# Attention and Sinkhorn-routed experts on one core: x kept by rows in DRAM and turned by DMA, weights in small loads

## The chip, the cores and the metric

The kernel runs on one core of one Trainium2 chip. The metric is the device time of one execution in microseconds (us). Three executions of the kernel before took 1023.87 us in the median (1021.98 to 1028.93). A further one was profiled, and every row below is from it.

## The reference

Attention over 8 batches with 8 heads of size 64: 512 local and 32 global tokens each. A local query sees the local keys within 32 positions and all global keys; a global query sees all keys. The result is x with N = 8*544 = 4352 rows and D = 512 columns. Then eight experts with weights from a Sinkhorn iteration:

```python
x = attn_out.transpose(0, 2, 1, 3).reshape(B * S, H * D)
P = np.exp(x @ w_gate - (x @ w_gate).max())
for _ in range(8):
    P /= P.sum(1, keepdims=True) + 1e-09
    P /= P.sum(0, keepdims=True) + 1e-09
    P *= N / E
for e in range(E):                      # E = 8, F = 1024
    h = np.maximum(x @ w1[e], 0.0)
    out += P[:, e:e + 1] * (h @ w2[e])
```

P depends on all rows of x, so no expert's share can be weighted before the attention of the last batch is done. Since P is positive, P * relu(x w1) w2 = relu((P x) w1) w2.

## The kernel before, in words

**Order of the work.** Every piece of work is an `op` with an engine, a cost in us, a key and dependencies (L123). `run_schedule` (L153) takes again and again the op that can start first by these costs, the smallest key first among equals, and issues it. So the order of instructions on each engine is fixed when the program is built, and each engine works through its own list in order: an instruction that waits holds all behind it on that engine. Loads and stores issued from SyncE stand in the queue SP, those from GpSimd in POOL.

**Attention** (L213 to L331). Work goes by 32 pairs of heads, four to a batch. Inputs of a batch are loaded on SP into single buffers (`load`, L202), cast by DVE, turned by PE (`transposes`, L222), and evicted; then scores, exponentials on ACT, masks on DVE, and `attend` (L268). `normalise` (L297) divides on DVE and writes x by rows, tokens on partitions. `back` (L329) turns the four 128x128 blocks of a pair with PE into the bank `xo`, and a copy (EB, L520) writes them into `xT`, a tile that holds all of x by columns in SBUF. The global rows go the same way by `flip` (L335, L526) and ACT (L527). `gate` (L339) makes the logits of all complete 128-row tiles after each batch, `exp_gate` their exponentials.

**Expert 0** (L388 to L422) runs unweighted and dense on groups of 512 tokens: `h_unit` makes the hidden layer, `y_unit` the second layer, `evac_y` copies it out, `store_y` (L422) stores it on POOL to `y0d` in DRAM. Its ops have keys from 1000 on, so PE takes them where attention leaves it free. Its weights are loaded by `load_w0` (L540).

**Sinkhorn** (L645 to L661) is a chain on DVE with a column sum on PE (L656) in each round. The result `P_nat` is turned by PE in three parts (`turn`, L667) and stored to `ptd`, so that it can be loaded back with the 256 tokens of a group along the free axis and spread over all partitions (`pb`, L696). x by columns is also stored, in 17 groups of 256 tokens (`xTd`, L610).

**Expert stage** (L818 on). Experts 1 to 7 run in two passes, (1, 2, 3) and (4, 5, 6, 7); a unit is one group of 256 tokens with one expert, 51 + 68 = 119 units. Both layers are done with seven products instead of eight (a Strassen-like scheme): the weights are combined by DVE (`combine_w1`, `combine_w2`, four operations of 128x1024 each), so is x (`prep`, L698). For each unit `prep` multiplies the group's x by `pb` (two DVE operations, L708) and makes three sums. Layer 1 of unit u (`add_layer1`, L847) is planned from TU*u on, TU = 6.2 us, and layer 2 (`add_layer2`, L880) two units later. Weighted x has three buffers (`xp`); unit k's buffer is that of unit k-3, whose last reader is product P3. Layer 2 accumulates over the experts of a pass in four PSUM banks; they start from the sum of the pass before (`load_o` L767, `seed` L773), which is stored by `store_o` (L935), both on SP.

The PSUM banks of the products of layer 1 come free with the attention pools (`open_late`, L614); those of layer 2 only when expert 0 is done (L808 to L815). All of the expert stage is planned after a first `run_schedule()` (L807) has issued attention, expert 0 and Sinkhorn.

**Weights** of experts 1 to 7 are loaded on POOL as four transfers each (`load_w1` L81, `load_w2` L89), fp32 in DRAM and fp16 in SBUF. Experts 1 and 2 are loaded near the end of attention, 3 when its pools are freed, 4 and 5 at unit 8 and 20 of the plan, 6 and 7 at the end of the first pass into the buffers of 1 and 2 (L956 to L961).

Of the kernel before, what the change touches and what calls it, by code (L numbers as in the profile page):

```python
# [9 lines left out]
FP16 = mybir.dt.float16  # L10
# [7 lines left out]
def kernel(  # L18
# [51 lines left out]
    identity32 = persist.tile([P, P], FP32)  # L70
    xT = fill.tile([P, DP, NTOK], FP16, bufs=1)
# [6 lines left out]
    xTd = dram.tile([GN, P, DP, 256], FP16)  # L78
    ws = {}

    def load_w1(e, pool, tag=""):  # L81
        w1r = pool.tile([P, 4, DK, F // 2], FP16, tag="w1r" + tag, bufs=1, name="w1r")
        src = moe_w1[e].rearrange("(dko dki) f -> dki dko f", dki=P)
        for f in (0, 1):
            nc.gpsimd.dma_start(out=w1r[:, 2 * f : 2 * f + 2].rearrange("p a k x -> p (a k) x"),
                                in_=src[:, :, F // 2 * f : F // 2 * (f + 1)])
        ws[e] = [w1r, None, None]

    def load_w2(e, pool, tag=""):  # L89
        wb = ws[e][1] = pool.tile([P, 7, FK, Dhalf], FP16, tag="wb" + tag, bufs=1, name="wb")  # L90
        src = moe_w2[e].rearrange("(fko fki) d -> fki fko d", fki=P)
        for c in (0, 1):
            nc.gpsimd.dma_start(out=wb[:, 2 * c : 2 * c + 2].rearrange("p a k x -> p (a k) x"),
                                in_=src[:, :, Dhalf * c : Dhalf * (c + 1)])
# [101 lines left out]
    qkT, ugk, u_, xns, ogs, pts, pss, pgs, pos_, pqs, hTs, phs, pys = ({} for _ in range(13))  # L196
# [100 lines left out]
    def normalise(p):  # L297
        pv = pos_[p][:, :, 0 : NM * VC].rearrange("p i (t c) -> p i t c", c=VC)
        rz = wk.tile([P, 2, NM], FP32, tag="rz", name="rz")
        nc.vector.reciprocal(out=rz, in_=pv[:, :, :, Dh])  # L300
        t = xns[p] = wk.tile([P, NM, 2, Dh], FP16, tag="xn", bufs=3, name="xn")
        nc.vector.tensor_tensor(out=t.rearrange("p t i d -> p i t d"), in0=pv[:, :, :, 0:Dh],
                                in1=rz.unsqueeze(3).broadcast_to([P, 2, NM, Dh]), op=ALU.mult)

    pog = gbank[:, 256 : 256 + VC]
    xo = gbank[:, 0:256].bitcast(FP16)
    ptg = gbank[:, 384 : 384 + 2 * Sg].rearrange("p (a s) -> p a s", s=Sg)
# [15 lines left out]
    def normalise_g(b, hh):  # L323
        rg = wk.tile([P, 1], FP32, tag="rg", name="rg")
        nc.vector.reciprocal(out=rg, in_=pog[:, Dh:VC])
        t = ogs[b, hh] = wk.tile([P, Dh], FP16, tag="og", name="og")
        nc.vector.tensor_scalar(out=t, in0=pog[:, 0:Dh], scalar1=rg[:, 0:1], scalar2=None, op0=ALU.mult)

    def back(p):  # L329
        for m in range(NM):  # L330
            nc.tensor.transpose(xo[:, P * m : P * (m + 1)], xns[p][:, m, :, :], identity)  # L331
# [7 lines left out]
    def gate(t0, t1):  # L339
        for to in range(t0, t1):  # L340
            for dk in range(DP):
                nc.tensor.matmul(pl[:, (to - t0) * E : (to - t0 + 1) * E], xT[:, dk, P * to : P * (to + 1)],
                                 w_gate_sb[:, dk, :], start=(dk == 0), stop=(dk == DP - 1))

    def exp_gate(t0, t1):
        nc.scalar.activation(out=K_nat[:, t0:t1, :].rearrange("p t e -> p (t e)"),
                             in_=pl[:, 0 : (t1 - t0) * E], func=AF.Exp)
# [37 lines left out]
    GT = 4  # L385
    groups = [(t, min(GT, TO - t)) for t in range(0, TO, GT)]

    def h_unit(g, fm, half):  # L388
# [6 lines left out]
        for dk in range(2 * half, 2 * half + 2):  # L395
            nc.tensor.matmul(phs[g, fm][:, 0:TG], w1_0[:, dk, P * fm : P * (fm + 1)], xT[:, dk, P * g0 : P * g0 + TG],  # L396
# [19 lines left out]
    def evac_y(eng, g, c):  # L416
        t = yss[g, c] = (late["ys"] if "ys" in late else fill).tile([P, D], FP32, tag="ys", bufs=5 if "ys" in late else 2,
# [8 lines left out]
    make_identity(nc, identity32)  # L426
# [22 lines left out]
    T, EQ, EK, SC, X, M, GK, XG, A, N, AG, NG, BK, EB, FL, EF, GA, GE, GO, XS = ({} for _ in range(20))  # L449
# [62 lines left out]
    def add_attend(p):  # L512
# [5 lines left out]
        N[p] = op("DVE", 0.85, lambda: normalise(p), k + 0.2, uses=[A[p]], alloc=("xn", 3))  # L518
        BK[p] = op("PE", 0.24, lambda: back(p), k + 0.3, uses=[N[p]], alloc=("xo", 1), lat=PEL)
        EB[p] = op(either(0.49, 0.61), 0, lambda eng: copy_on(eng, xT[:, hp, S_tok * b + Sg : S_tok * (b + 1)], xo), k + 0.3,  # L520
                   uses=[BK[p]])
        if hp % 2 == 1:
            AG[b, hh] = op("PE", 0.36, lambda: attend_g(b, hh), k + 0.25, [A[p], XS[b // 2]],
                           uses=[X[p, 0, 0], X[p - 1, 0, 0]], alloc=("pog", 1), lat=PEL)
            NG[b, hh] = op("DVE", 0.4, lambda: normalise_g(b, hh), k + 0.25, uses=[AG[b, hh]], alloc=("og", 2))
            FL[b, hh] = op("PE", 0.15, lambda: flip(ptg, ogs[b, hh]), k + 0.35, uses=[NG[b, hh]], alloc=("ptg", 1), lat=PEL)  # L526
            EF[b, hh] = op("ACT", 0.15, lambda: nc.scalar.copy(  # L527
                out=xT[:, 2 * hh : 2 * hh + 2, S_tok * b : S_tok * b + Sg], in_=ptg), k + 0.35, uses=[FL[b, hh]])

    S_tok = Sg + Sl  # L530
# [7 lines left out]
    tick = const.tile([P, 1], FP32)  # L538

    def load_w0():  # L540
        nc.gpsimd.tensor_copy(out=tick, in_=stage[1, "q"][:, 0, 0:1])
# [6 lines left out]
    ready_b, sched_gate = {}, 0  # L548
    for b in range(B):
# [17 lines left out]
        t0, t1 = sched_gate, (S_tok * (b + 1)) // P  # L567
        sched_gate = t1
        ready_b[b] = [EB[p] for p in range(HP * b, HP * (b + 1))] + [EF[b, 0], EF[b, 1]]
        GA[b] = op("PE", 0.55, lambda t0=t0, t1=t1: gate(t0, t1), HP * (b + 1) + 0.6, ready_b[b], alloc=("pl", 1), lat=PEL)  # L570
# [424 lines left out]
```

## Time and profile before

| what | value |
|---|---|
| profiled execution | 1021.38 us |
| its span | 1019.7 us, mean granted clock 0.99 |
| last gate's exponential starts | 187.9 us |
| P_nat written | 219.6 us |
| first product of the expert stage | 260.6 us |
| last matmul starts | 1013.6 us |
| DMA packets | 127530, 119.18 MB |
| SP's queue (hardware) | 91.13 MB, 29.3% of the 16 engines' span |
| POOL's queue (software) | 25.70 MB, 13.4% |

In the 40 slices of the profile each slice is 25.5 us and each digit a tenth of busy time. PE's busy time counts matmuls with modelled, overlapping ends; the weight loads (PEld) take about 0.1 us each and tell better how dense PE's work is. Attention fills slices 0 to 7, the rest of expert 0 with Sinkhorn beside it 7 to 10, the expert stage the remainder.

### The profile page before, as it was taken

How to read it: one execution, taken by the hardware profiler on the slowest of the kernel's cores; microseconds unless marked ns; L12 is line 12 of the kernel's file. 1: busy time of each engine (PE TensorE's matmuls, PEld its weight loads, DVE VectorE, ACT ScalarE, POOL GpSimd, SP SyncE). 2: the span in 40 equal slices, each digit the busy share in tenths (PEclk: the TensorE clock that was granted, in tenths of full speed). 3: DMA queues.
4: the chain of work that ended last, by engine and by line, in shares of the span. 5: the costliest groups of instructions: out<-in, count | busy, mean ns of one | idle time of the engine just before them, and what ended most of it. 6: DMA issues, size and time to landing. Idle time of an engine off the chain costs nothing. (4 is left out here: it accounts for less than half of the span.)

```text
span 1019.7 us, 30644 instructions
## 1 busy us (share of the span) xinstructions
PE 980.2 (96%) x12921; PEld 829.9 (81%) x12921; DVE 884.6 (87%) x2058; ACT 671.7 (66%) x1306; POOL 51.8 (5%) x89
## 2 busy tenths in 40 slices
PE   5999999889999999999999889999999999999997
PEld 3556555434799999999999878999999999999997
DVE  5577776581599999999999899999999999999996
ACT  4678877434677766676776656666666666666664
POOL 2000130211300000000000100000000000000000
PEclk9799999989999999999999999999999999999999
DMA  9979696732962232232322891222222222222211
GB/s 272 256 219 307 193 215 126 144 103 100 229 140 85 94 94 89 90 94 93 108 73 79 153 195 60 88 73 74 74 74 73 75 74 74 74 75 73 75 43 43
DMA packets 127530, 119.18 MB, mean 117 GB/s; under 512 B 17424, under 2 KB 102944, under 8 KB 127392
## 3 DMA queue, kind: packets, MB, share of 16 engines
q1 hardware_dynamic: 99040, 91.13, 29.3%
q0 software_dynamic: 26768, 25.70, 13.4%
q8 instruction: 101, 1.65, 0.7%
q10 hardware_dynamic: 1584, 0.39, 0.2%
q14 instruction: 37, 0.30, 0.1%
HBM read 102.65 MB, written 31.33 MB: 131 GB/s over the span
## 5 line engine op out<-in xcount | busy, mean ns | idle before, releaser
L740 ACT ACTIVATE h<-h 128x512 f16<-128x512 f16 x357 | 224.2, 630 | 72.0 <-DVE h L100 70.1
L726 PEld LDWEIGHTS <-w1r 128*128 128x128 f16 x3808 | 244.9, 98 | 22.6 <-issue 13.7
L726 PEld LDWEIGHTS <-w1x 128*128 128x128 f16 x2856 | 182.3, 98 | 5.3
L764 PEld LDWEIGHTS <-s 128*128 128x128 f16 x1904 | 172.4, 98 | 15.9 <-DVE s L100 0.6
L708 DVE TENSOR_TENSOR xp<-xg,pb 128x512 f16<-128x512 f16 x238 | 163.0, 686 | 15.2 <-PE Y L726 15.0
L726 PE MATMUL X<-tt,w1r 128*128 128x128 f16 x1904 | 145.1, 219 | 7.4 <-ACT u3s L737 5.8
L764 PE MATMUL acc_4639<-wb,s 128*128 128x256 f16 x952 | 142.5, 273 | 0.3 <-DVE s L100 0.3
L764 PEld LDWEIGHTS <-h 128*128 128x128 f16 x1428 | 130.0, 98 | 12.6 <-issue 1.0
L737 ACT COPY u3s<-X 128x512 f32<-128x512 f32 x119 | 69.4, 583 | 73.7 <-PE X L726 73.4
L100 DVE TENSOR_TENSOR h<-p1s,Z 128x512 f16<-128x512 f32 x119 | 81.0, 681 | 29.5 <-ACT p1s L737 27.9
L737 ACT COPY p1s<-X 128x512 f32<-128x512 f32 x119 | 69.1, 580 | 29.1 <-PE X L726 29.1
L100 DVE TENSOR_TENSOR h<-u3s,Y 128x512 f16<-128x512 f32 x119 | 81.1, 681 | 2.1 <-ACT u3s L737 2.1
L737 ACT COPY u2s<-X 128x512 f32<-128x512 f32 x119 | 68.5, 576 | 21.5 <-PE X L726 21.4
L100 DVE TENSOR_TENSOR h<-u2s,Y 128x512 f16<-128x512 f32 x119 | 81.0, 680 | 1.6 <-PE Y L726 1.6
L740 ACT ACTIVATE h<-X 128x512 f16<-128x512 f32 x119 | 70.1, 589 | 17.0 <-PE X L726 14.0
L396 PE MATMUL ph<-xT,w_0_77 128*128 128x512 f16 (+1 forms) x288 | 74.0, 374 | 1.8 <-ACT ys L200 1.1
L726 PE MATMUL X<-xp,w1r 128*128 128x128 f16 x952 | 72.6, 219 | 1.9 <-DVE xp L708 1.7
L726 PE MATMUL Z<-xp,w1r 128*128 128x128 f16 x952 | 72.6, 219 | 1.1 <-DVE h L100 1.0
L726 PE MATMUL X<-tt,w1x 128*128 128x128 f16 x952 | 72.6, 219 | 0.0
L726 PE MATMUL Y<-tt,w1x 128*128 128x128 f16 x952 | 72.6, 219 | 0.0
L726 PE MATMUL Y<-xp,w1x 128*128 128x128 f16 x952 | 72.6, 219 | 0.0
L764 PE MATMUL acc_4636<-wb,s 128*128 128x256 f16 x476 | 71.4, 273 | 0.1
(985 smaller groups left out, 1651.1 us busy)
## 6 DMA issues: line engine op xcount, KB each, us to landing
pb<-ptd SPq DMA_DIRECT2D x119, 128.0 KB, 4.1
y0d<-ys POOLq DMA_DIRECT2D x34, 256.0 KB, 3.5
xg<-xTd SPq DMA_DIRECT2D x34, 256.0 KB, 3.7
o<-y0d SPq DMA_DIRECT2D x34, 256.0 KB, 2.8
ya<-o SPq DMA_DIRECT2D x34, 256.0 KB, 2.1
o<-ya SPq DMA_DIRECT2D x34, 256.0 KB, 3.0
out_dram<-o SPq DMA_DIRECT2D x34, 256.0 KB, 2.0
qs<-in_q_l_dram SPq DMA_DIRECT2D x7, 1024.0 KB, 6.9
```

The source lines that it names most:

```text
L100: nc.vector.tensor_tensor(out=o, in0=a, in1=b_, op=ALU.add)
L396: nc.tensor.matmul(phs[g, fm][:, 0:TG], w1_0[:, dk, P * fm : P * (fm + 1)], xT[:, dk, P * g0 : P * g0 + TG], start=(dk == 0), stop=(dk == ...
L708: nc.vector.tensor_tensor(out=x[:, ks], in0=xgs[n, g][:, ks], in1=pb.unsqueeze(1).broadcast_to([P, DK, 256]), op=ALU.mult)
L726: nc.tensor.matmul(dst[:, j, :], l[:, d, P * j : P * (j + 1)], r[:, d, :], start=(first and j == 0 and d == 0), stop=(j == FK - 1 and d == ...
L737: nc.scalar.copy(out=d[k], in_=X[k])
L740: nc.scalar.activation(out=hq(k, f, t), in_=hq(k, f, t) if src is None else src, func=AF.Relu)
L764: nc.tensor.matmul(acc(i), l[:, j, :], wb[:, r, j, :], start=(e == es[0] and j == 0 and i in (1, 5)), stop=(e == es[-1] and j == FK - 1), ...
```

## The change

x is no longer kept by columns in SBUF. `normalise` writes two pairs into one tile, which POOL stores by rows to `xd` in DRAM (`store_x`), the global rows SP (`store_xg`). For gate and expert 0 each group of 512 tokens is read back with a DMA transpose on SP (`turn_group`), into three buffers; gate goes by these groups. In the expert stage a group is loaded by rows once per pass, scaled by rows with P as a scalar per partition on ACT or DVE (`scale_x`), stored to one of four DRAM buffers (`put_x`), and read back with a DMA transpose (`turn_x`). P is not turned any more.

Weights of experts 1 to 5 are loaded on POOL in 16 pieces each; before each piece POOL waits until the piece before the last has landed. In the expert stage each piece also waits for the x of a given unit. Experts 6 and 7 are first converted to fp16 in DRAM by 16 pieces each and then loaded by SP in four halves. `load_o` and `store_o` move from SP to POOL, the third seed of a group is placed after the second. Layer 1 of units 0 and 1 and the x of units 0 to 3 are planned in the first `run_schedule()`, together with expert 0.

```diff
+    def load_piece(e, i):
+        if len(landed) > 1:
+            wait_for(landed[-2])
+        if i < 8:
+            k, f = divmod(i, 2)
+            o = ws[e][0][:, 2 * f + k // DK, k % DK, :]
+            nc.gpsimd.dma_start(out=o, in_=moe_w1[e][P * k : P * (k + 1), F // 2 * f : F // 2 * (f + 1)])
+            landed.append(o[:, 0:1])
...
+    def cast_piece(e, i):
+        d, src, n = (wd1, moe_w1, D // 8) if i < 8 else (wd2, moe_w2, F // 8)
+        r = slice(n * (i % 8), n * (i % 8 + 1))
+        nc.gpsimd.dma_start(out=d[e][r], in_=src[e][r])
...
-    def back(p):
-        for m in range(NM):
-            nc.tensor.transpose(xo[:, P * m : P * (m + 1)], xns[p][:, m, :, :], identity)
+    def store_x(b, hh):
+        r0 = S_tok * b + Sg
+        nc.gpsimd.dma_start(out=xd[r0 : r0 + Sl, 4 * Dh * hh : 4 * Dh * (hh + 1)].rearrange("(m p) d -> p m d", p=P),
+                            in_=xns[2 * b + hh].rearrange("p m i d -> p m (i d)"))
...
+    def turn_group(g):
+        t0, n = groups[g]
+        xTs[g] = fill.tile([P, DP, n * P], FP16, tag="xT", bufs=3, name="xT")
+        nc.sync.dma_start_transpose(out=xTs[g], in_=xd[P * t0 : P * (t0 + n)])
...
-        BK[p] = op("PE", 0.24, lambda: back(p), k + 0.3, uses=[N[p]], alloc=("xo", 1), lat=PEL)
-        EB[p] = op(either(0.49, 0.61), 0, lambda eng: copy_on(eng, xT[:, hp, S_tok * b + Sg : S_tok * (b + 1)], xo), k + 0.3,
+            stored[b].append(op("DMA3", 0.7, lambda: store_x(b, hh), k + 0.5, uses=[N[p], N[p - 1]], lat=DMAL))
...
+                TG[g] = op("DMA", 2.0, lambda g=g: turn_group(g), k, [x for x in stored[b] + (stored[b - 1] if b else [])],
+                           alloc=("xT", 3), lat=5.5)
+                GA[g] = op("PE", 0.55, lambda g=g: gate(g), k + 0.1, alloc=("pl", 1), uses=[TG[g]], lat=PEL)
...
-        t = pbs[n, g] = late["cp"].tile([P, 4, 2, P], FP32, tag="pb", name="pb")
-        for i, e in enumerate(es):
-            nc.sync.dma_start(out=t[:, i], in_=ptd[2 * g : 2 * g + 2, e, :].unsqueeze(0).broadcast_to([P, 2, P]))
+    def scale_x(eng, k, a):
...
+        if eng == "ACT":
+            nc.scalar.activation(out=o, in_=i, func=AF.Copy, scale=w)
+        else:
+            nc.vector.tensor_scalar(out=o, in0=i, scalar1=w, scalar2=None, op0=ALU.mult)
+    def put_x(k):
+        nc.sync.dma_start(out=xsd[k % NX].rearrange("(a p) d -> p a d", p=P), in_=xss[k])
+    def turn_x(k):
+        xps[k] = late["cp"].tile([P, DP, 256], FP16, tag="xp", bufs=3, name="xp")
+        nc.sync.dma_start_transpose(out=xps[k], in_=xsd[k % NX])
...
-            nc.vector.tensor_tensor(out=x[:, ks], in0=xgs[n, g][:, ks], in1=pb.unsqueeze(1).broadcast_to([P, DK, 256]),
...
+        mk("PX", k, "DMA", 0.1, lambda: put_x(k), at + 1.0, [(("SC", 1), k)], [(("SC", 0), k)], ("xsd", NX), lat=2.3)
+        mk("TX", k, "DMA", 1.2, lambda: turn_x(k), at + TU, [], [("PX", k)], ("xp", 3), lat=2.3)
...
-                    mk("FC", nx, "ACT", 0.4, lambda: seed(*nx, 2), t + 9.0, [], [("LO", nx)])
+                    mk("FC", nx, "ACT", 0.4, lambda: seed(*nx, 2), t + 12.0, [("FA", nx)], [("LO", nx)])
...
-        mk("LO", c, "DMA", 0.2, lambda: load_o(*c), t, alloc=("o", 2), lat=2.5)
+        mk("LO", c, "DMA2", 1.5, lambda: load_o(*c), t, [("open", 0), ("y", 0), ("y", 1)], alloc=("o", 2), lat=6.0)
...
+    def load_w(e, deps, pool):
+        for i in range(16):
+            mk(("W", i), e, "DMA", 1.3, lambda i=i: (new_w(e, i, pool()), load_piece(e, i)), 900.0 + e + 0.01 * i,
+               deps if i == 0 else [(("W", i - 1), e)], lat=DMAL)
...
+    for k in range(4):
+        add_prep(k)
+    add_o(c0, 0.0)
+    for k in (0, 1):
+        add_layer1(k)
+    run_schedule()
...
+        if 4 <= u < NW:
+            add_prep(u)
+            while npc < 64 and 4 + npc * 0.66 <= u:
+                add_piece(npc, u)
+                npc += 1
```

## The prediction

> **What bounds the kernel now.** I read the page first (busy times, 40 slices), then busy time by stretch, the groups by shape, the timeline of 187 to 260 us, the waits of 500 to 570 us and the DMA issues.
>
> ```profile
> span 1019.7 us, 30644 instructions
> PE 980.2 (96%) x12921; PEld 829.9 (81%) x12921; DVE 884.6 (87%) x2058; ACT 671.7 (66%) x1306; POOL 51.8 (5%) x89
> PE   5999999889999999999999889999999999999997
> PEld 3556555434799999999999878999999999999997
> ```
>
> PE is the bound nearly everywhere; the weight loads (PEld) show where it is full in earnest: from slice 10 on, with a dip at slices 22 to 24 (about 560 to 640 us).
>
> ```profile
> 26.00:60.00 34.00, 30.95 (x468) 19.37 (x465) 22.50 (x55) 22.63 (x50) 0.40 (x1) 0.85 0.86 224
> 200.00:210.00 10.00, 5.30 (x17) 2.15 (x17) 7.01 (x17) 1.67 (x3) 0.54 (x1) 0.70 0.70 147
> 300.00:400.00 100.00, 99.91 (x1349) 93.55 (x1347) 100.00 (x237) 70.25 (x133) 0.00 (x0) 1.00 0.30 94
> 500.00:570.00 70.00, 65.51 (x884) 61.48 (x883) 63.02 (x151) 45.65 (x89) 1.50 (x2) 1.00 0.28 88
> 570.00:650.00 80.00, 75.47 (x996) 69.10 (x993) 79.02 (x183) 49.18 (x94) 4.99 (x6) 1.00 0.60 123
> 700.00:800.00 100.00, 100.00 (x1363) 94.89 (x1361) 95.26 (x225) 67.91 (x127) 0.00 (x0) 1.00 0.24 75
> ```
>
> Columns: stretch, length, PE, PEld, DVE, ACT, POOL busy with counts, granted clock, DMA share, GB/s. A unit of the expert stage has 7*8 + 7*4 = 84 matmuls; at 1363 per 100 us it takes 6.17 us, and 119 units 734 us. The stage runs from 260.4 to 1014.2, 754 us, so about 20 us are lost in it: against 13.63 per us, 300-500 lacks 2.8 us, 500-570 5.1, 570-650 6.9, the rest lies in the first 40 us and the drain.
>
> ```profile
> 202.26 0.44 DVE L643 TENSOR_TENSOR t_4156<-K_nat,rv 128x272 f32<-128x272 f32 x1
> 204.90 0.69 DVE L97 TENSOR_TENSOR wb<-wb 128x1024 f16<-128x1024 f16 x1 [2.19 <-DMA wb<-in_moe_w_dram]
> 205.51 0.62 DVE L651 TENSOR_REDUCE cp<-t_4156 128x8 f32<-128x272 f32 x1
> ...
> 206.19 0.59 PE L656 MATMUL pcs<-cp,ones_sc 128*128 128x8 f32 x2 [3.83 <-DVE cp L651]
> ```
>
> Here one weight combination stands in DVE's queue before its data, the Sinkhorn step behind it is late, and PE, in order, stands for 3.83 us at the column sum although expert 0 has work; the clock is then 0.50 from 205 to 210.
>
> ```profile
> L331 PE MATMUL gbank<-identity,xn 128*128 128x128 f16 x128 | 13.3, 230 | 3.6 <-DVE og L327 1.7 <-DVE xn L302 1.7
> L337 PE MATMUL gbank<-identity,og 128*64 128x64 f16 x32 | 3.6, 218 | 0.5 <-ACT xT L200 0.2
> L200 ACT COPY xT<-gbank 128x512 f16<-128x512 f16 x30 | 17.7, 590 | 10.0 <-PE gbank L337 6.0 <-PE gbank L331 3.8
> ...
> ACT o L781 <- DMA o<-y0d: 9.3, 4, 4.0
> ...
> PE X L726 <- ACT u3s L737: 4.5, 4, 3.0
> ...
> y0d<-ys POOLq DMA_DIRECT2D x34, 256.0 KB, 3.5
> xg<-xTd SPq DMA_DIRECT2D x34, 256.0 KB, 3.7
> xTd<-xT SPq DMA_DIRECT2D x17, 256.0 KB, 5.4
> ...
> w1r<-in_moe_w_dram POOLq DMA_DIRECT2D x14, 512.0 KB, 8.9
> wb<-in_moe_w_dram POOLq DMA_DIRECT2D x14, 512.0 KB, 13.3
> ```
>
> Groups, waits (500-570), DMA issues (last number: us to landing). The first are what the change takes off PE and ACT.
>
> **The change, part by part** (against the profiled execution: 1021.4, that is 1019.7 of span and 1.7 around it; it lies 2.5 us under the median of 1023.9).
>
> 1. *Back transposes and flips go.* In the timeline four transposes hold PE from 100.02 to 100.30 and 110.15 to 110.43, about 0.28 us, a flip pair 0.16 (176.05 to 176.21): 32*0.28 + 16*0.16 = 11.5, with the three turns of P (0.3 each) 12 us. PE is full from 60 us on (40.00 of 40 in 100-140), so all counts: **-12**. ACT's copies (30*0.59 + 16*0.22 = 21 us) are hidden beside PE and are counted at nothing; without that cover they would be a gain.
> 2. *Weights of experts 1-3 in 48 small loads.* POOL waits for the piece before the last, so two are in flight. Nearest rows: 256 KB store on POOL 3.5 us, 512 KB load 8.9, so 1.75 to 4.5 us a piece. From 130 us (before's first load goes out at 128) experts 1 and 2 are in after 32 pieces at 186 to 274. I take the low end, the same size on a quiet queue: DMA share falls to 0.29 at 160-180 once q, k, v are in. Then the stand at 204.9 goes: 3.83 and about 2 of the slow clock, **-6**; high end under the rivals. Expert 3's 16 pieces follow: w1 is due for unit 2, after 250, and is there by 230. Queued on POOL behind the waits are y0d and x stores; at 1.75 a wait, the five y buffers cover it.
> The Trainium skill (DMA: Bandwidth & Descriptors, Anatomy of one DMA and Measured) speaks against this part: it fits 2.0 us + bytes/436 GB/s and advises 1 MiB or more. As an estimate by that page 256 KB take 2.6 us, two in flight 1.3, 48 pieces 62 us, against 53 for twelve of 1 MiB at 4.4; the term would not change.
> 3. *Pass 1's y0d loads go to POOL with more lead, and the third seed moves behind the second.* ACT's four waits of 9.3 us cost PE 4.5: **-4.5**.
> 4. *Switch to experts 6, 7.* DVE is full at 570-650 (79.0 of 80): 16 combinations of 0.69. The change takes two multiplies of 0.686 off DVE per unit and adds two scalings, at most 0.42 (row of the 128x512 f16 operations) and possibly on ACT: 0.5 to 1.4 us free per unit, for some six units 3 to 8 of the 11 us. The loads become half as large (f16 already in DRAM). Of 6.9 us I take **-4** (range 0 to -7), and of the 2.8 at 300-500, where DVE is at 100.00, **-1.5**.
> 5. *First two units' layer 1 beside expert 0.* PE work is conserved (2*7*0.44 = 6.2 us): only ramp holes are filled, **-2**.
> 6. *Later x for gate and expert 0.* Now: store on POOL (0.54 issue, 3.5 landing), a wait on SP, transpose, gate. No row shows a DMA transpose. Nearest for 512 KB: the 256 KB store from the same queue and stage, 2.6 to 12.6, median 5.4, and 13.3 for a 512 KB weight load. So x arrives 0.5+3.5+(2.6 to 13.3) = 7 to 17 us after normalisation. Expert 0 starts then, not at 43.2 but some 10 us later: lost are about 14 matmuls of 0.216 (28 run in 40-60): **+3** (0 to +6). Each gate is placed in PE's order by the planner's charges, 0.7+2.2 for the store and 2.0+5.5 for the turn, 10.4 in all; PE stands where the chip is later, 0 to 6.6 us for each of some eight groups, 0 to 53. I take **+5**, since the nearest row (5.4) puts the chain at the charge and only the tail over it. SP, in order, stands at the turn for the store: behind it are q, k, v loads, but before's last one (v of batch 7) goes out at 127, 40 us ahead of use.
> Three buffers of x also force expert 0 forward: for the last gate layer 1 of group 5 must be done, 192 matmuls; by 188 some 160 have run. With the y units between that is 66*0.216 = 14 us earlier, not more, work.
> 7. *Sinkhorn later.* Attention's end moves 187 - 11 (part 1 without the turns of P) + 14 = 190; with 11 for store, turn and gate Sinkhorn starts at 201, takes 28 (eight rounds of 3.19 and 2) and ends at 229; scaling 0.6, store 3.1, turn 5: unit 0's x at 238. Expert 0 ends at 260.4-12-6+8 = 250, so 12 us are left to hide layer 1 of two units. Cover thin: **+3** (0 to +12).
> 8. *Every unit's x by store and turn.* Steady state is PE's. The buffer of unit k is free when P3 of unit k-3 ends, 2*6.17-3.9 = 8.4 us before P1 of unit k; turn issue and landing 0.4+3.7 fit (as xg), 0.4+8.9 would miss by 0.9. I take 3.7, the same bytes on the same queue: **0**, high end 119*0.9 = 107. Bytes per unit: 256 KB out, 256 in, 85 group, 340 o and ya, up to 390 weights, 1.33 MB in 6.17 us = 215 GB/s at most, against 258 moved in the first 100 us at a share near 0.94.
> The Trainium skill (Advanced Engine Details and Errata, X-Bar Transpose (TRN2)) holds transposes as fast as copies, 350 to 400 GB/s; by an estimate from it 256 KB take 0.7 us and this term stays 0. No row here shows it.
>
> **Sum**: -12-6-4.5-4-1.5-2 = -30, +3+5+3 = +11: -19, 1021.4-19 = **1002**.
>
> **Rivals.**
> - *Time goes into new waits of the same size.* Weights at the upper 4.5 us a piece hold DVE's combinations inside Sinkhorn (experts 1, 2 only at 274), or x at 17 us holds its start: each us past the 12 of cover counts. With 20 us, 1022. For it: exactly that wait stands at 204.9 now. Against: DMA share 0.29 at that time.
> - *The gates hold PE in attention* (slower). Place: PE in front of each gate, 30 to 190 us. At the upper 6.6 us times eight, +53 for my +5: 1050, with part 7's upper end 1059. From 24/8 = 3 us over the charge per group it is no gain. For it: DMA share 0.86 to 0.94 at 26-100 and landings up to 12.6. Against: the median 5.4.
> - *The turn is too slow for three buffers* (slower): at 8.9 us, 1002+107 = 1109; it decides from 8.4+0.2 us of issue and landing. For it: no row shows the operation. Against: 3.7 us for the same bytes.
> - *The overlap does not come about* since unit 0's x is after expert 0's end: costs part 5 and up to 9 more, 1013; inside the first case's range.
>
> **How the numbers follow.** A measurement of this kernel (1022.0 to 1028.9) tells about 1% from no change, 1013.6 to 1034.1. Forecast 0.52 (own range 985 to 1013.5: the gains without any of the +11, 991, less the upper ends of parts 3 to 5, some 6, up to the lost overlap); new waits 0.13 (1014 to 1034); gates 0.20 (1034 to 1060); slow turn 0.15. Faster 0.52, same 0.13, slower 0.35. Leaving out the slow turn and 0.05 under 985, the range is 985 to 1060.
>
> **What would show it.** Parts 1, 6: no L331-like transposes in attention, gate matmuls' idle before them under 1 us each; waits on x there prove the gates' rival. Part 2: no idle of PE over 2 us at the column sum. Part 7: first unit's product before expert 0's last y. Parts 3, 4: over 1340 matmuls per 100 us between 480 and 620. Part 8: product P1 waiting for the turned x in each unit would prove it wrong.

## The result and the profile after

The changed kernel takes 1101.36 us (median of 4 runs, 1096.79 to 1106.05) against 1025.13 for the kernel before beside it (1021.98 to 1028.93): a ratio of 1.0742, 95% interval 1.0682 to 1.0802. It is slower; the forecast of 1002 and its range of 985 to 1060 both missed. The profiled execution took 1101.87 us, 1100.1 of it span.

First the page of the changed kernel (busy times; PE and PEld in 40 slices):

```profile
span 1100.1 us, 31180 instructions
PE 993.8 (90%) x12758; PEld 830.6 (75%) x12758; DVE 794.8 (72%) x1954; ACT 716.6 (65%) x1360; POOL 214.8 (20%) x465
PE   6798998797989889988898989999999999999996
PEld 4454554344788778888887888889999998999995
```

PE has 163 instructions fewer than before and is still the busiest engine, but in the expert stage, where PEld stood at 9 in nearly every slice, it is now at 7 and 8 up to slice 26 (about 740 us). Busy time by stretch (stretch, length, PE, PEld, DVE, ACT, POOL, granted clock, DMA share, GB/s):

```profile
26.00:60.00 34.00, 24.53 (x362) 16.55 (x359) 21.65 (x50) 14.91 (x31) 2.68 (x4) 1.00 0.94 230
300.00:400.00 100.00, 88.34 (x1165) 81.22 (x1163) 76.84 (x192) 70.67 (x132) 31.60 (x80) 1.00 0.81 156
400.00:500.00 100.00, 86.75 (x1132) 80.14 (x1130) 72.30 (x180) 70.89 (x134) 32.81 (x75) 0.98 0.81 163
500.00:570.00 70.00, 63.90 (x830) 58.99 (x829) 51.19 (x130) 50.25 (x95) 17.77 (x41) 0.98 0.77 163
700.00:800.00 100.00, 95.33 (x1281) 89.23 (x1280) 79.10 (x201) 68.61 (x127) 8.56 (x16) 1.00 0.54 130
```

At 84 matmuls a unit, 1165 per 100 us are 7.2 us a unit in place of 6.17. No engine is full there: PE 88, DVE 77, ACT 71, DMA share 0.81. So this is waiting, not work, and the waits say for what. DVE's waits from 300 to 600 us (total, times, longest):

```profile
DVE tt L126 <- DMA xp<-xsd_82: 16.2, 5, 4.3
...
DVE tt L126 <- DMA xp<-xsd_80: 13.8, 6, 4.2
DVE tt L126 <- DMA xp<-xsd_81: 9.2, 5, 2.9
DVE tt L126 <- DMA xp<-xsd_79: 8.0, 7, 3.5
```

That is 47 us of 300 in which DVE stands at the first subtraction of a unit until its turned x has landed. SP's queue in the same stretch (L720 is the store of the scaled rows):

```profile
SPq L720 <- ACT xs L715: 94.0, 29, 8.1
SPq L720 <- DVE xs L717: 56.5, 18, 7.3
SPq L724 <- PE Y L747: 30.3, 28, 4.2
SPq L720 <- DVE tt L126: 29.0, 5, 6.8
```

SP stands 180 us at the store, waiting for scaled rows. One turn of the wheel, from the timeline (start, us, engine, line, operation, in brackets the idle time before it):

```profile
405.91 0.38 SPq L720 DMA_DIRECT2D xsd_81<-xs  x1
...
407.03 1.23 SPq L724 DMA_TRANSPOSE xp<-xsd_79  x1
...
409.05 0.42 DVE L126 TENSOR_TENSOR tt<-xp 128x512 f16<-128x512 f16 x1 [4.33 <-DMA xp<-xsd_82]
...
411.18 1.23 ACT L761 ACTIVATE h<-h 128x512 f16<-128x512 f16 x2 [4.48 <-DVE h L129]
...
414.97 0.71 ACT L715 ACTIVATE xs<-xg,P_nat 128x512 f16<-128x512 f16 x1
415.18 0.35 DVE L717 TENSOR_SCALAR xs<-xg,P_nat 128x512 f16<-128x512 f16 x1
...
415.71 0.38 SPq L720 DMA_DIRECT2D xsd_82<-xs  x1
...
416.89 1.23 SPq L724 DMA_TRANSPOSE xp<-xsd_80  x1
```

DVE stands 4.33 us for one unit's turn. ACT, which needs a sum that is behind it in DVE's list, stands 4.48 us. The scalings of a later unit come after both, its store is ahead of the next turn in SP's list, and so the next turn goes out 9.9 us after the last one, where a unit has 6.17.

The other part of the loss lies ahead of the expert stage: PE has 24.53 us of work between 26 and 60 us (30.95 before), the first product of expert 0 is at 61.3 us (43.2), Sinkhorn runs from 233.4 to 262.9 (188 to 220), and the last product of expert 0 ends at 289.2 (259.7). PE also stands before two of the nine gates until the group's turned x has landed, 10.9 us in all (PE's timeline, L386 is the gate):

```profile
189.45 0.57 PE L386 MATMUL gbank<-w_gate_sb,xT 128*128 128x8 f16 x16 [3.74 <-DMA xT<-xd]
...
216.49 0.59 PE L386 MATMUL gbank<-w_gate_sb,xT 128*128 128x8 f16 x16 [7.18 <-DMA xT<-xd]
```

### The profile page after: what moved, and what is told of

Its sections match the earlier page's. It is cut to its first block, busy times and chain, and to the rows that moved or that the text cites. A ratio compares the mean times of both kernels' runs of the same rounds, so it can differ in the third digit from the quotient of the medians.

```text
span 1100.1 us, 31180 instructions
## 1 busy us (share of the span) xinstructions
PE 993.8 (90%) x12758; PEld 830.6 (75%) x12758; DVE 794.8 (72%) x1954; ACT 716.6 (65%) x1360; POOL 214.8 (20%) x465
## 2 busy tenths in 40 slices
DMA packets 263071, 174.53 MB, mean 159 GB/s; under 512 B 164752, under 2 KB 250000, under 8 KB 262416
## 4 chain that ended last, share of the span: by engine, by line
PE 33%; DMA 15%; DVE 6%; issue 5%; SPq 1%; ACT 1%; POOL 0%; POOLq 0%; DVEq 0%; ACTq 0%
PE X L747 9%; PE Y L747 5%; PE acc_4690 L785 5%; PE acc_4691 L785 5%; PE acc_4688 L785 4%; DMA xp<-xsd_80 4%; DMA xg<-xd 4%; DMA xp<-xsd_82 3%; DMA xp<-xsd_81 3%; PE Z L747 2%; PE acc_4689 L785 2%; DVE h L129 2%; DVE tt L126 1%; SPq L724 1%; DMA xp<-xsd_79 1%
## 5 line engine op out<-in xcount | busy, mean ns | idle before, releaser
L747 PEld LDWEIGHTS <-w1r 128*128 128x128 f16 x3808 | 250.5, 98 | 21.7 <-issue 10.9
L747 PEld LDWEIGHTS <-w1x 128*128 128x128 f16 x2856 | 188.4, 98 | 27.9 <-issue 20.3
L785 PEld LDWEIGHTS <-s 128*128 128x128 f16 x1904 | 168.0, 98 | 51.0 <-DVE s L126 28.0
L785 PE MATMUL acc_4691<-wb,s 128*128 128x256 f16 x952 | 143.4, 273 | 32.4 <-DVE s L126 24.4
L126 DVE TENSOR_TENSOR tt<-xp 128x512 f16<-128x512 f16 x119 | 50.2, 422 | 89.3 <-DMA xp<-xsd_82 34.2
L947 POOL DMA_DIRECT2D out_dram<-o x34 | 18.6, 548 | 328.1 <-DVE tt L129 280.2
L715 ACT ACTIVATE xs<-xg,P_nat 128x512 f16<-128x512 f16 x100 | 71.4, 721 | 11.0 <-DMA xg<-xd 9.5
L785 PE MATMUL acc_4688<-wb,h 128*128 128x256 f16 x476 | 72.6, 276 | 0.5
```

The source lines that it names most:

```text
L126: nc.vector.tensor_tensor(out=o, in0=a, in1=b_, op=ALU.subtract)
L715: nc.scalar.activation(out=o, in_=i, func=AF.Copy, scale=w)
L747: nc.tensor.matmul(dst[:, j, :], l[:, d, P * j : P * (j + 1)], r[:, d, :], start=(first and j == 0 and d == 0), stop=(j == FK - 1 and d == ...
L785: nc.tensor.matmul(acc(i), l[:, j, :], wb[:, r, j, :], start=(e == es[0] and j == 0 and i in (1, 5)), stop=(e == es[-1] and j == FK - 1), ...
L947: nc.gpsimd.dma_start(out=(ya, outr)[c[0]][2 * c[1] + a], in_=obs[c][:, a, :])
```

## The experiments

All ratios are to the kernel before, run on the same chip.

| kernel | median us | ratio, 95% interval |
|---|---|---|
| changed kernel | 1101.36 | 1.0742, 1.0682 to 1.0802 |
| e1: no weight loads in the stage | 1071.19 | 1.0440, 1.0416 to 1.0464 |
| e2: store from ACT | 1125.5 | 1.0952, 1.0895 to 1.1009 |
| e3: four buffers of turned x | 1112.63 | 1.0852, 1.0807 to 1.0897 |
| e4: one turn for each group | 1036.54 | 1.0116, 1.0071 to 1.0160 |
| e5: longer landings planned, 4.0 and 6.5 us | 1060.77 | 1.0367, 1.0319 to 1.0415 |
| e7: e5, scaling and store on ACT, four buffers | 1080.19 | 1.0569, 1.0515 to 1.0624 |
| e9: e4, global rows stored by POOL | 1036.05 | 1.0136, 1.0088 to 1.0184 |
| e10: before with the weight part alone | 1028.63 | 1.0058, 1.0035 to 1.0081 |
| e11: e10, combinations later | 1036.68 | 1.0124, 1.0094 to 1.0154 |
| e12: before with the y0 lead alone | 1016.16 | 0.9929, 0.9901 to 0.9956 |
| e13: e5, landings ahead of the stage too | 1055.83 | 1.0308, 1.0271 to 1.0345 |
| e14: e4, four turned groups | 1038.99 | 1.0144, 1.0109 to 1.0180 |
| e15: e13 without the stage's weight loads | 1032.47 | 1.0091, 1.0062 to 1.0121 |
| e16: e13, four buffers of turned x | 1049.49 | 1.0242, 1.0199 to 1.0284 |
| e17: e13, group loads earlier, a third buffer for them | 1033.86 | 1.0100, 1.0069 to 1.0132 |
| e18: before, expert 0 one batch later | 1034.62 | 1.0118, 1.0095 to 1.0141 |

**First round: which link of the store and turn?** Theory A: the turn stands behind a later unit's store in SP's list. B: three buffers are too few. C: the weight loads make the landings long.

*e1*, the stage's paced weight loads, late halves and combinations left out (experts 4 to 7 compute with the tiles of experts 1 to 3, so part of the computation is changed):

```diff
-            while npc < 64 and 4 + npc * 0.66 <= u:
+            while npc < 0:
...
+    for e in (4, 5, 6, 7):
+        ws[e] = ws[(e - 1) % 3 + 1]
```

> The changed kernel without any weight load in the expert stage: experts 4 to 7 run with the tiles of experts 1 to 3 (so their share of the output is another), the 64 pieces, the four late halves per expert and the combinations of experts 4 to 7 are left out. Theory C (the pieces crowd the DMA engines and make each turned x land late): the units up to about 600 us run as fast as those after it now do, 6.35 us instead of 7.2 over 46 units, so 35 to 45 us less, about 1060. Theory A (the turn stands in SP's list behind the store of a later unit) and theory B (three buffers of x give too short a window): the list and the window are as before, at most 15 us less, mostly from DVE's missing combinations, 1086 or more. The 23 us lost before the stage stay under all three.

It gave about 30 us back: more than A and B expected, less than C. The weight loads have a share, but the stage loses without them too.

*e2*, the store issued from ACT's queue:

```diff
-        nc.sync.dma_start(out=xsd[k % NX]...
+        nc.scalar.dma_start(out=xsd[k % NX]...
...
-        mk("PX", k, "DMA", 0.1, ...
+        mk("PX", k, "ACT", 0.1, ...
```

> The changed kernel with the store of the scaled x (put_x) issued from ScalarE's queue and no longer from SP, so that on SP only group loads, turns and the late weights stand. Theory A: the 380 us of waits of put_x on SP hold no turn any more, 35 to 50 us less, 1050 to 1066. Theory B: the turn still waits for its buffer, which comes free as before, at most 10 us less or a few more for ScalarE's issue time. Theory C: as B.

It became slower, so A falls as it was posed. DVE's stand is what it was (waits of 300 to 600 us):

```profile
DVE tt L126 <- DMA xp<-xsd: 46.9, 20, 5.6
```

and the store now stands in front of ACT's own work (timeline; ACT's next copy comes 3.53 us late because of the store ahead of it, which needs the other half of the rows, scaled elsewhere):

```profile
424.25 0.71 ACT L715 ACTIVATE xs<-xg,P_nat 128x512 f16<-128x512 f16 x1
428.07 0.38 ACTq L720 DMA_DIRECT2D xsd<-xs  x1
428.49 0.59 ACT L758 COPY u2s<-X 128x512 f32<-128x512 f32 x1 [3.53 <-issue]
```

*e3*, a fourth buffer, and the turn planned 3.2 us earlier:

```diff
-        xps[k] = late["cp"].tile([P, DP, 256], FP16, tag="xp", bufs=3, name="xp")
+        xps[k] = late["cp"].tile([P, DP, 256], FP16, tag="xp", bufs=4, name="xp")
...
-        mk("TX", k, "DMA", 1.2, lambda: turn_x(k), at + TU, [], [("PX", k)], ("xp", 3), lat=2.3)
+        mk("TX", k, "DMA", 1.2, lambda: turn_x(k), at + 3.0, [], [("PX", k)], ("xp", 4), lat=2.3)
```

> The changed kernel with four buffers of turned x instead of three, each turn planned half a unit earlier: the window from a buffer's release to its first use grows by a unit, 8.4 to 14.6 us. Theory B: 40 to 55 us less, 1046 to 1061, and no waits of the sums on the turned x. Theory A: the turn is still behind the store in SP's list, 15 us less at most. Theory C: the longer landings fit into the longer window too, so 30 to 50 less as well; the first run tells B and C apart.

Slower than the changed kernel, and DVE still waits 44.3 us for turned x; B falls for the orders planned here (e16 asks it again).

*e4*, x turned once for each group and pass from the unscaled rows (34 turns in place of 119), multiplied by DVE with P turned and spread as in the kernel before; weights and everything ahead of the stage as changed:

```diff
+        x = xgs[n, g] = late["cp"].tile([P, DP, 256], FP16, tag="xg", name="xg")
+        nc.sync.dma_start_transpose(out=x, in_=xd[256 * g : 256 * (g + 1)])
...
+            nc.vector.tensor_tensor(out=x[:, ks], in0=xgs[n, g][:, ks], in1=pb.unsqueeze(1).broadcast_to([P, DK, 256]),
+                                    op=ALU.mult)
```

> The changed kernel with the x of the units prepared as before the change: P turned by TensorE and spread by loads, x turned once per group and pass straight from the rows in DRAM (34 turns in place of 119 stores and 119 turns), then two multiplies on DVE per unit. All theories on the units' x: what the stage lost goes, about 57 us, less a few for DVE: 1045 to 1055. What then stays over the kernel before, about 20 us, is lost before the stage. If it stays above 1080, the units' x is not the cause, and the moved stores and loads of the sums or the pieces are.

The stage is at its full rate, weight loads and all (windows of e4):

```profile
26.00:60.00 34.00, 23.19 (x384) 16.03 (x381) 21.76 (x51) 15.06 (x32) 2.69 (x4) 0.72 0.98 235
300.00:400.00 100.00, 100.00 (x1368) 94.79 (x1366) 99.41 (x236) 71.25 (x135) 41.48 (x92) 1.00 0.63 125
```

So the units' stores and turns, as they are planned in the changed kernel, cost about 65 us in all (1101.4 - 1036.5), and the first line shows the second loss unchanged.

**Second round.** With A and B down, a new theory, D: the ring shown above, made by the planner. It lays down each engine's order from its own charges, and it charges 2.3 us of landing for the store and 2.3 for the turn, where the trace has 2.2 to 7.5 and 3.2 to 8.0. (The trace counts from the start of the issue, with medians of 3.6 and 4.6; the planner's charge with its issue, 0.1 and 1.2 us, is 2.4 and 3.5.) It therefore puts a unit's subtraction on DVE where the x has not landed.

*e5* changes two numbers of the planner:

```diff
-        mk("PX", k, "DMA", 0.1, ..., ("xsd", NX), lat=2.3)
-        mk("TX", k, "DMA", 1.2, ..., ("xp", 3), lat=2.3)
+        mk("PX", k, "DMA", 0.1, ..., ("xsd", NX), lat=4.0)
+        mk("TX", k, "DMA", 1.2, ..., ("xp", 3), lat=6.5)
```

> As the changed kernel, but the planner that lays down every engine's order is told that a store of the scaled rows takes 4.0 us and a turn 6.5 us to land, in place of 2.3 us for each (the trace shows 2.2 to 7.5 and 3.2 to 8.0 us between 300 and 600 us). Theory D: the units lose their time in a ring of in-order queues: DVE stands at the first subtraction of unit k until its turned x has landed, the scaling of unit k+2 is behind it in DVE's list, the store of unit k+2 waits for that scaling at the head of SP's list, and the turn of unit k+1 is behind that store. Orders made with the measured landings put the scaling ahead of the subtraction, and half or more of the 65 us that the units' stores and turns cost comes back: 1070 us or less. Theory B2: the turn can't start before a third-last unit gives up its buffer, whatever the order: within 10 us of the changed kernel, 1091 to 1111 us. Theory C: the landings are long from the traffic beside them: 1091 to 1111 us too.

About 40 us come back, as D expected. The new charges are 4.1 and 7.7 us with the issue, so above the medians, and for the turn near the longest landing; whether the medians themselves would do was not run. DVE's wait for the turned x between 300 and 600 us has gone from 47 us to

```profile
DVE tt L126 <- DMA xp<-xsd: 2.0, 3, 1.3
```

though the turns land no sooner; the DMA issues of the changed kernel (one of its four DRAM buffers; the others have 4.2, 4.4 and 5.4) and of e5 in that stretch (last number: median us to landing):

```profile
xp<-xsd_80 SPq DMA_TRANSPOSE x11, 4.6
```

```profile
xp<-xsd SPq DMA_TRANSPOSE x46, 4.8
```

*e7* takes everything of a later unit out of DVE's and SP's lists: `scale_x` on ACT alone, `put_x` from ACT, four buffers and turns planned 3.2 us earlier, landings as in e5.

> As the changed kernel with the ring cut at every link: both halves of x scaled by ACT, the store issued from ACT's queue right behind them, so that neither DVE's list nor SP's has anything of a later unit ahead of a turn; four buffers for the turned x, turns planned 3.2 us earlier, and landings planned as 4.0 and 6.5 us. ACT gets about 0.4 us more work for each unit (0.72 us in place of 0.35 on DVE), at 70 us of 100 busy. Theory D (ring) and theory B2 (buffers): most of the 65 us back, 1037 to 1060 us. Theory C (traffic): landings stay 4 to 8 us and the gain is small, 1080 us or more.

Faster than the changed kernel, but slower than e5, and just where C expected it. ACT waits 31.7 us in 14 waits for the group's rows (7.6 us in the changed kernel), with all its other work behind them. That a wait moved to an engine with a long list costs more there is read from these rows: e7 differs from e5 in the scaling, the store's queue, the buffers and the turns' places, and none of them was run alone.

*e9* is e4 with `store_xg` on POOL's queue.

> As the run with one turn per group (1036.5 us), but the four small stores of each batch's global rows are issued from POOL's queue and not from SP's. Theory F1: the loads of q, k and v of batches 2 and later stood on SP behind those stores (issued at 37 us, 15 to 25 us in the kernel before), so PE had 24.5 us of work in 26 to 60 us where it had 31: 6 to 12 us less, 1025 to 1031 us. Theory F2: attention was held by the transposes into x and by the buffers of the turned x, which this leaves alone: 1033 to 1040 us.

No change; F1 falls. The loads of batch 1 are back at 15.7 to 26.3 us (15.0 to 25.4 in the kernel before, 37.0 to 38.5 in the changed kernel). SP now stands at the turn itself (SP's waits, 20 to 200 us):

```profile
SPq L382 <- DMA xd<-og: 68.8, 9, 18.6
```

but the loads of batch 2 that stand behind it go out at 51.8 and 52.5 us, and they went out at 46.1 and 54.3 in the kernel before, where buffers held them.

*e10* puts the weight part on the kernel before: the pieces, the conversions and halves of experts 6 and 7, and the y0 loads and stores on POOL.

> The kernel before (x turned by TensorE, kept whole in SBUF, first units after the routing) with only the change's treatment of weights and of the stores beside them: experts 1 to 3 in 48 small loads, experts 4 and 5 in paced small loads, 6 and 7 through cast copies in DRAM, the y0 loads and output stores on POOL's queue with the lead of 6.0 us, and the third seed after the second. Theory W: my prediction's parts 2, 3 and 4 were right and each stands for itself: 6 us at the column sum, 4.5 us at the late y0, 4 to 5.5 us at the switch, so 1009 to 1015 us. Rival: these gains came from the new x path, or the small loads take as much elsewhere: 1020 to 1030 us.

The three gains together made it 0.6% slower. Where the stand at the column sum was to vanish it is longer (windows, then timeline of e10):

```profile
188.00:200.00 12.00, 2.90 (x14) 1.19 (x12) 3.29 (x8) 1.78 (x3) 6.00 (x14) 0.78 0.83 169
```

```profile
197.65 0.69 DVE L126 TENSOR_TENSOR wb<-wb 128x1024 f16<-128x1024 f16 x1 [8.71 <-POOL tick L93]
...
199.89 0.60 PE L684 MATMUL pcs<-cp,ones_sc 128*128 128x8 f32 x2 [9.10 <-DVE cp L679]
```

The 32 pieces of experts 1 and 2 go out between 125.5 and 195.5 us, 2.26 us each, and a combination stands in DVE's list before its piece: the same stand as before, 9.1 us in place of 3.8.

**Third round.** *e11* is e10 with a piece planned as 2.4 us and the combinations of the second weights held until the routing is done:

```diff
-            W[e, i] = op("DMA", 1.3, ...
+            W[e, i] = op("DMA", 2.4, ...
...
-            op("DVE", 0.605, lambda n=n: combine_w2(e, n), key, [W[e, i] for i in range(8, 16)])
+            op("DVE", 0.605, lambda n=n: combine_w2(e, n), 1.2 + 0.1 * e, [W[e, i] for i in range(8, 16)] + [chain[-1]])
```

> As the run with the weight part alone (1028.6 us), where DVE stood 8.7 us in the column sums' stretch at a combination of expert 1's second weights whose last piece landed at 197 us. Here the planner is told 2.4 us for a piece in place of 1.3 us (the trace shows one piece in about 2.0 us) and these combinations are held until the routing is done, when DVE has 26 of 30 us free in the kernel before. Theory W2: the stand was all that ate the gains; TensorE's 9.1 us stand at the column sum goes, 1012 to 1020 us, below the kernel before. Rival: the combinations then delay the stage's first units (DVE has 34.5 us of work in the 40 us from 260): 1021 to 1030 us.

The column sum's stand goes, and the time is given back at 260 us and more (waits, 250 to 290 us):

```profile
DVE wb L126 <- DMA wb<-in_moe_w_dram: 19.1, 2, 10.6
...
PE Z L754 <- DVE h L129: 15.9, 1, 15.9
DVE w1x L129 <- DMA w1r<-in_moe_w_dram: 15.4, 1, 15.4
```

The 48th piece goes out only at 266.3 us. At this rate the small loads of expert 3 are late for a stage that begins at 260 us. In the changed kernel, whose stage begins later, DVE waits 1.4 us for them.

*e12* is the kernel before with two numbers changed:

```diff
-                    mk("FC", nx, "ACT", 0.4, lambda: seed(*nx, 2), t + 9.0, [], [("LO", nx)])
+                    mk("FC", nx, "ACT", 0.4, lambda: seed(*nx, 2), t + 12.0, [("FA", nx)], [("LO", nx)])
...
-        mk("LO", c, "DMA", 0.2, lambda: load_o(*c), t, alloc=("o", 2), lat=2.5)
+        mk("LO", c, "DMA", 0.2, lambda: load_o(*c), t, alloc=("o", 2), lat=6.0)
```

> The kernel before with only the planner's numbers for the y0 loads changed: 6.0 us of landing in place of 2.5 us, and the third seed behind the second. Queues, weights and x as before. If my prediction's 4.5 us (TensorE's four waits for ACT's u3s between 500 and 650 us) came from those loads alone: 4 to 5 us less, a ratio of 0.995 to 0.996. If it took the move to POOL's queue or the paced weights: no change, 0.998 to 1.002.

It beats both kernels: a ratio of 0.9929 (0.9901 to 0.9956), somewhat more than expected, 7.9 us between the medians, and 4.3 us between the profiled spans, 1015.4 against 1019.7. The stretch is now full, and TensorE's waits for u3s are gone from it:

```profile
500.00:570.00 70.00, 70.00 (x950) 66.38 (x948) 68.59 (x162) 51.45 (x96) 1.50 (x2) 1.00 0.37 100
```

*e13* is e5 with the landings ahead of the stage planned as well (9.0 us for the stores of x's rows, 7.5 for the turns of a group).

> As the run with planned landings (1060.8 us; ratio 1.037), and in the stage before too the planner is told what the traces show: 9.0 us for the stores of x's rows in place of 2.2 us, 7.5 us for the turns for gate and expert 0 in place of 5.5 us. Theory F4: orders made with short landings put loads and products behind turns that have not landed; 5 us or more less, 1046 to 1056 us. Theory F3: what is lost there is work that does not exist yet (expert 0's products start at 61 us, 43 us in the kernel before) and a last turn that waits for one of three buffers: 1057 to 1065 us.

The time lies in F4's range, but the intervals of e5 and e13 overlap: some 6 us, not settled.

*e14* is e4 with four buffers of turned groups and three of y.

> As the run with one turn per group (1036.5 us; ratio 1.0116), with four buffers for the turned x of gate and expert 0 in place of three (and three for y in place of five, for room). Theory F3: the last group's turn waits for a buffer that expert 0 frees one group (8 to 9 us) earlier, the last gate comes at about 222 us and not 237, Sinkhorn ends so much earlier, and the stage starts 5 to 10 us earlier: 1027 to 1032 us. Rival: expert 0's own end (about 280 us, with no work in its place) sets the stage's start: 1034 to 1039 us.

The last gate comes 18 us earlier (e4: 237.5 us; ACT's timeline of e14):

```profile
219.32 0.18 ACT L392 ACTIVATE K_nat<-gbank 128x16 f32<-128x16 f32 x1
```

and the time does not fall. F3 falls: the late gate and the late Sinkhorn are beside expert 0's end, not on the path (its last product ends at 286.4 us, in e4 at 286.0). Two things stay open in this run: three buffers of y may have cost something, and TensorE still stands 11.3 us before gates (14.4 in e4).

**Last round: what is left of the stage, and of the time ahead of it.** *e15* is e13 with e1's edit.

> As the run with all landings planned (1055.8 us; ratio 1.0308), and the paced weight loads, late halves and combinations of experts 4 to 7 left out (experts 4 to 7 compute with the tiles of 1 to 3, so part of the computation is changed). It asks what the units' store and turn still cost when the orders fit the landings. Theory C (the weight loads' traffic and their waits on the turned x): 15 to 22 us less, 1034 to 1041 us, as leaving them out took 30 us off the changed kernel. Rival (buffers, or ACT's and DVE's added work): at most 6 us less, 1050 us or more.

Some 22 us back, as C expected, though C's way (long landings) is not it, as e17 shows. *e16* is e13 with four buffers for the turned x:

> As the run with all landings planned (1055.8 us), with four buffers for the turned x in place of three. Theory B2: SP's turns still wait 77 us in 39 waits for TensorE's last read of a buffer; with a fourth the turns go out up to a unit earlier and 8 us or more comes back: 1048 us or less. Rival: those waits lie beside the other waits of SP (118 us for scaled rows) and cost nothing: 1052 to 1059 us.

Between the two expectations, and the intervals of e13 and e16 overlap. *e17* is e13 with the loads of a group's rows planned two units earlier, into a third buffer (`bufs=3` for `xg`), and at 5.0 us of landing:

```diff
-            mk("LG", k, "DMA", 0.1, lambda: load_group(n, g), at - TU, [("open", 0)], alloc=("xg", 2), lat=2.5)
+            mk("LG", k, "DMA", 0.1, lambda: load_group(n, g), at - 3 * TU, [("open", 0)], alloc=("xg", 3), lat=5.0)
```

> As the run with all landings planned (1055.8 us), with each group's rows loaded two units earlier into a third buffer and planned as 5.0 us of landing. ACT waited 16.3 us in 10 waits for those rows between 300 and 600 us. If these waits pass on to the store and the turn: 6 to 15 us less over the whole stage, 1040 to 1050 us. If ACT has the time: 1053 to 1059 us.

More than expected, 22 us, with the weight loads in place and with three buffers of turned x. The stage is now at its full rate with a store and a turn for every unit (windows of e17):

```profile
300.00:400.00 100.00, 99.69 (x1353) 94.18 (x1351) 89.30 (x228) 78.10 (x149) 35.98 (x90) 1.00 1.00 185
500.00:570.00 70.00, 70.00 (x956) 66.42 (x953) 60.43 (x157) 53.65 (x101) 17.45 (x40) 1.00 0.88 187
700.00:800.00 100.00, 100.00 (x1362) 94.89 (x1361) 78.67 (x197) 79.84 (x150) 8.66 (x16) 1.00 0.58 141
```

More is moved than in the changed kernel (185 GB/s against 156, DMA share 1.00 against 0.81), and the turns land in the same 4.8 us. The transport was not too slow for this rate; it was asked for too late. Which of the three changes to the group loads gave the 22 us was not run.

*e18* is the kernel before with expert 0's products held until the next batch is complete:

```diff
-            u0 = op("PE", us, ..., key, [w0, *ready_b[min(g, B - 1)], before],
+            u0 = op("PE", us, ..., key, [w0, *ready_b[min(g + 1, B - 1)], before],
```

> The kernel before, with expert 0's first product of each group of 512 rows held until the rows of the next batch are complete too, some 15 to 20 us later than now; nothing else is changed (x by TensorE, all of it in SBUF). In the changed kernel and all runs built on it that product starts at 60 to 61 us, in the kernel before at 43.2 us, and the stage before the experts ends about 19 us later. Theory F5: expert 0's products are what TensorE does between two pieces of attention, and starting them 18 us later leaves it idle then and late at the end: 8 to 18 us more, 1031 to 1041 us. Rival: attention takes up the time and expert 0 only ends in another order: within 4 us of the kernel before; then the loss is in the turns' and gates' own waits.

F5 holds: 1.2% slower, spans 1032.5 against 1019.7. The first product starts at 55.9 us (43.2 before, 61.3 in the changed kernel), and the last one of expert 0 ends at 270.2 (259.7). Windows of e18 (PE alone, granted clock, DMA share, GB/s), against 30.95 us before:

```profile
26.00:60.00 34.00, 28.96 (x438) 0.66 0.91 232
```

## Why the prediction was wrong

The spans differ by 80.4 us. Of these 67.8 lie between the changed kernel and e17, so in the orders of the expert stage and a third buffer for the group's rows (with whatever e13's two numbers ahead of the stage gave: expert 0 ends at 277.7 us in e17, at 289.2 in the changed kernel). The other 12.6 are what is lost ahead of the stage less the gain of part 3.

- **Part 8, every unit's x by store and turn, taken as 0: the step that failed.** It cost about 65 us. Its sum was near: a turn takes 4.6 us from the start of its issue to landing, for my 4.1. (Landings count from the start of the issue, so the 1.23 us of issue are in the 4.6, and I should not have added 0.4 to the 3.7, nor 0.5 to the 3.5 in part 6.) The longest is 8.0 us, within the 8.4 us that a buffer leaves, and e17, with turns of up to 8.9 us, runs at full rate on three buffers. Also the bytes were right (at most 215 GB/s by my sum, 185 to 192 moved in e17). What failed was to take "the buffer's window fits" as enough. The order of DVE's, ACT's and SP's lists is fixed by the planner from landings of 2.3 us. I had held the planner's charges against the landings in part 6 and not here. A charge below the chip's time puts an engine in front of data that is not there, and behind it stands what the next transfer needs. The sign that I named for this part, a unit's first product waiting for the turned x, hardly shows it: TensorE has 5.4 us of idle time before these products (X<-xp) in the whole run of the changed kernel. It was DVE that stood.
- **Rival "the turn is too slow for three buffers" (0.15, 1109)** had nearly the time by luck, and not the mechanism: the turn took 4.6 us, at most 8.0, under the 8.6 from which it was to decide, a fourth buffer made the changed kernel no faster (e3), and under e13's orders its gain is not settled (e16).
- **Part 6, later x for expert 0, +3: mis-sized.** The start came 18 us later, not 10. In e18, where only expert 0's products are held and the first comes 12.7 us later, the cost is 12.8 us between the profiled spans and 11.0 between the medians: TensorE's idle time between pieces of attention wasn't made up later. The turn of a group lands in 4.1 to 12.7 us, median 7.5, within my 2.6 to 13.3. The gates' +5 was too small as well: TensorE stands 3.74 and 7.18 us before two gates, where my sign asked for under 1 us before each. The gates' rival, a stand before each of them and +53, did not come about: the other seven show none in the changed kernel. What the two stands cost was not run; e14 moves the last gate by 18 us and keeps 11.3 us of them.
- **Part 7, +3:** the times were off by a lot (Sinkhorn at 233 and not 201, expert 0's end at 289 and not 250) for the reason of part 6; with both late, Sinkhorn's end is not the path (e14).
- **Part 2, -6:** no stand of over 1 us remains at the column sum in the changed kernel, but there Sinkhorn starts 45 us later. On the kernel before it is longer (e10), and then moves to expert 3's weights (e11). The piece took 2.26 us (2.33 in the changed kernel), in my range of 1.75 to 4.5, and the low end that I chose decided the sign. The first rival's mechanism was right here. The Trainium skill (DMA: Bandwidth & Descriptors, Anatomy of one DMA) led to an estimate of 1.3 us a piece; the measurement decides for 2.3.
- **Part 3, -4.5: right**, 4.3 us between the spans in e12, 7.9 between the medians. The move to POOL was not needed for it; the lead and the third seed's place, changed together, were enough.
- **Part 4, -4 and -1.5:** PE has 75.45 to 75.47 us of work in 570 to 650 us in the kernel before, in e10 and in e12, and 75.60 in e17, where DVE is relieved (68.3 of 80): the -4 did not come. This does not clear the full DVE as a cause of the dip before, since e17 has another dip. Before, DVE is busy 9.9 us or more of each 10 from 570 to 640; in e17 most of the loss lies in 600 to 610 (PE 6.08 of 10, DVE 6.97), where DVE waits 3.86 us for a half of a late expert's weights. At 300 to 500 us e17 has 2710 matmuls for 2687, 1.7 us, and e4, e10 and e12, where DVE is still full, 2685 to 2691: the -1.5 was right.
- **Part 1, -12:** the instructions are gone, but PE is idle in that stretch (72.1 of 80 us in 60 to 140 in e17, 78.8 before), so it can't be read from the time. **Part 5, -2:** the first unit's product (271.0 us) does run beside expert 0's last (289.2); its worth wasn't tried.

Left open: e18 accounts for 11 to 13 us of the loss ahead of the stage. With part 1's gain counted there should be more to find. TensorE's stands before gates (10.9 us in the changed kernel, 9.6 in e17) are one candidate and planned landings (e13) another; no run prices either. Why e2 and e7, which cut links of the ring, did worse than e5 is read from ACT's waits and wasn't tried further.

## What to carry to other kernels

Where a planner writes the orders of in-order queues, hold its charge for each new transfer against the landing time in a trace first: two short charges cost 40 us here, and group loads planned too late on two buffers 22 more, while the engines and the DMA had room. A window of buffers that fits a transfer says only that it can be in time; what stands ahead of its issue on each queue says whether it is. And work that fills the gaps of another stage is not free to start later: in e18 a later start of 12.7 us cost 11 to 13 us.

## What the runs showed of the hardware

- A DMA transpose of 256 x 512 fp16 holds SP's queue for 1.23 to 1.41 us (medians of the four buffers), where the store of the same bytes holds it for 0.38, and lands in 4.6 us from the start of its issue (3.2 to 8.0), the stores of the same stretch in medians of 2.7 to 3.9. The Trainium skill (Advanced Engine Details and Errata, X-Bar Transpose (TRN2)) has transposes as fast as copies; in these rows they take about 1 us longer to land, 4.6 us against 3.6.
- The changed kernel moves 174.5 MB in 263071 packets, 164752 of them under 512 bytes (119.2 MB, 127530 and 17424 before). In spite of that e17 keeps PE full at a DMA share of 0.85 to 1.00.
- Of the kernels with the change, the clock granted between 26 and 60 us was 0.67 to 0.72 in some (e2 to e5, e7, e9), with 384 to 409 matmuls done there, and 1.00 in others (changed kernel, e16, e17), with 362 to 365. In this stretch, where PE waits, the higher clock did not go with more work.
